# Attention, gated product and routed experts in one kernel: q and k transposed by head pairs, scores on half-array rows, and moved steps in the opening and around the last routing

## The chip, the cores and the metric

The kernel runs on one core of one Trainium2 chip. The metric is device time in microseconds (us), from the start of one execution to its end; the reference's arithmetic is all done in one launch.

## What is computed

Three blocks follow one another, in f32: attention with a sliding window of 128 and four sink tokens (4 batches, 8 heads, 768 tokens, head size 64), a gated product, and eight experts of which each token uses one.

```python
keep = (pos_k < 4) | ((rel >= 0) & (rel < 128))          # sinks, or inside the window
a = softmax(where(keep, q @ k.T / sqrt(64), -1e9))        # (4, 8, 768, 768)
x = (a @ v) as (3072, 512)                                # heads side by side
x = (((x @ w1) * (x @ w2)) @ w3) @ w_out                  # 512 -> 1024 -> 1024 -> 512; weights are f64
e = argmax(x @ w_gate + modality_bias[modality_id])       # one of 8 experts a token
out = gate * (relu(x @ e_w1[e]) @ e_w2[e])                # 512 -> 1024 -> 512
```

## The kernel before

All products keep f32 accuracy by a split: a number is a high part in f32r and a low part (what is left), and a product is high x high, high x low and low x high, three matmuls of 512 columns where one would stand. The five engines are TensorE (PE), VectorE (DVE), ScalarE (ACT), GpSimd (POOL) and SyncE (SP), which issues most transfers.

**Opening** (`front`, `startup_stream`). The f64 weights come in through SP into four tiles `f64st` (`f64_load`), DVE turns them into f32 (`f64_to_f32`), PE transposes w3 (L280), ACT and a correction matmul with `neg_r` split the result (`split_bank`, L266 to L268), and PE multiplies w3 by w_out into eight tiles `w3o` (L289). Attention steps are put between.

**Attention.** The work is 48 pairs n: 12 units u of 256 tokens (batch b, chunk c of 3) by 4 head pairs p. For each pair:
- `a_load`, `a_load_v`: q, k and v from DRAM;
- `a_split`: ACT makes the high parts of q and k, DVE the low parts, in SBUF;
- `a_tq`, `a_tk` (L396, L415): for each of head and half unit PE transposes a 128x128 block that holds high and low part side by side, so that high and low lie on rows 0 to 63 and 64 to 127; `a_swap` writes a second q with the two exchanged;
- `a_scores(n, j)` for the two half units j: two matmuls of 264 columns a head (two blocks of 128 keys and 4 sinks), with q and swapped q, over all 128 rows (L441). DVE masks and takes the maximum, ACT the exponential, `norm` (DVE) divides;
- `a_sk`: POOL collects the sink columns in `psk` and PE transposes them (L492);
- `a_pt`: PE transposes the probabilities in f32 (L504), ACT evicts, POOL masks;
- `a_pv`: PE multiplies by v in f32, 64 output columns a head (L531; an f32 matmul is two passes in the trace), adds the sinks (L534), and ACT and DVE split the result into `xb`.

**moe1_stream** runs six groups `gr` of two units: `ab` products (L703, w1 and w2, 16 groups of 12 matmuls), `x2` products (L691), and the `late` half of them. `front` puts attention steps of the next group between its steps, by a model time t, and steps of `route` (16 reductions on DVE, L764, then the expert's choice, its rank, and the tables) for the units already done. In the last group attention is over, and the slots of the experts start: a `Slot` is 512 tokens of one expert; `decide` picks it on DVE (some 16 small operations) and SP loads the result into registers, since the addresses of the slot's weights and tables depend on it.

**back** works the slots off: `stage1` (L912), `stage2` (L949), the weight pieces of the next slot (`w1_piece`, `w2_piece`: SP load L868 or L870, split on ACT L195 and DVE L196) and its transposes (L899).

The order of the instructions of an engine follows from the code's order and from a scheduler, which moves an instruction up where it judges its operands ready; `high_priority` moves a stretch forward. Each engine then works its own list in order.

Of the kernel before, what the change touches and what calls it, by code (L numbers as in the profile page):

```python
# [26 lines left out]
def attention_moe_moe_kernel(ctx, tc, q, k, v, w1, w2, w3, w_out, mod_id, w_gate, mod_bias, e_w1, e_w2, out,  # L27
# [18 lines left out]
    banded = n_sink == NS and window == 128  # L46

# [46 lines left out]
    neg_r = const.tile([128, 128], F32R, name="neg_r")  # L94
    cur_i = const.tile([128, 128], I32, name="cur_i")
# [12 lines left out]
    ksk = const.tile([128, H, NS], F32R, name="ksk")  # L108
# [3 lines left out]
    def consts_early():  # L112
# [5 lines left out]
        nc.vector.tensor_scalar(out=neg_r, in0=idf, scalar1=-1.0, scalar2=None, op0=ALU.mult)  # L118
        nc.gpsimd.memset(tmp, 1.0)
# [217 lines left out]
    carry = {}  # L337
    xb = mm.tile([128, NP, 2, 3, UNIT], F32R, tag="xb", bufs=1, name="xb")

    def a_load(n):  # L340
# [3 lines left out]
        qn = att.tile([128, 2, 2, D], F32, tag="qn", bufs=2, name="qn")  # L344
        kn = att.tile([128, 2, 2, D], F32, tag="kn", bufs=2, name="kn")
        for src, dst in ((q, qn), (k, kn)):
            for j in range(2):
                s0 = c * UNIT + j * 128
                nc.sync.dma_start(out=dst[:, :, j], in_=src[b, hs, s0:s0 + 128, :].rearrange("h s d -> s h d"))
        nat[n] = (qn, kn)  # L350

    def a_load_v(n):
# [8 lines left out]
        if c == 0 and p == 0:  # L361
            for kind in range(3):
                for h in range(2):
                    r = kind * 32 + h * NS
                    nc.sync.dma_start(out=vst[r:r + NS, :, h * D:(h + 1) * D],
                                      in_=v[b].rearrange("(p h) s d -> h s p d", h=2)[h, 0:NS])
# [7 lines left out]
    def a_split(n):  # L374
        qn, kn = nat.pop(n)
        qs = att.tile([128, 4, 2, D], F32R, tag="qs", bufs=1, name="qs")
        ks = att.tile([128, 4, 2, D], F32R, tag="ks", bufs=1, name="ks")
        qf = qn.rearrange("p h j d -> p (h j) d")
        kf = kn.rearrange("p h j d -> p (h j) d")
        nc.scalar.activation(out=qs[:, :, 0, :], in_=qf, func=ACTF.Copy, scale=1.0 / float(D) ** 0.5)  # L380
        nc.scalar.activation(out=ks[:, :, 0, :], in_=kf, func=ACTF.Copy)

        def low_parts():
            nc.vector.scalar_tensor_tensor(out=qs[:, :, 1, :], in0=qf, scalar=1.0 / float(D) ** 0.5,
                                           in1=f32(qs[:, :, 0, :]), op0=ALU.mult, op1=ALU.subtract)
# [23 lines left out]
    def a_tk(n):  # L409
# [9 lines left out]
        if c == 0:  # L419
            nc.gpsimd.tensor_copy(out=ksk[:, 2 * p:2 * p + 2, :], in_=f32(kT[:, :, 1, NS:2 * NS]))  # L420
# [794 lines left out]
```

## Time and profile before

| | us |
|---|---|
| median of 3 runs (1012.55 to 1014.28) | 1012.94 |
| the profiled execution | 1017.59 |
| its span | 1015.9 |

| engine | busy, us | share of the span | instructions |
|---|---|---|---|
| PE, matmuls | 956.0 | 94% | 4976 |
| PE, weight loads (beside matmuls) | 752.5 | 74% | 4976 |
| DVE | 644.0 | 63% | 1968 |
| ACT | 515.8 | 51% | 1354 |
| POOL | 218.0 | 21% | 460 |

Busy time is the union of an engine's instructions. A matmul's record is longer than what it costs: the next one starts before it ends, so the cost of a group is read from start to start. Whose wait ends last is told by the view of waits; an idle engine that nobody waits for costs nothing.

### The profile page before, as it was taken

Reading aid. Unit: us, or ns where it says so; the run is one execution under the profiler, and the core shown is the slowest. Engines: PE = TensorE matmul, PEld = TensorE weight load, DVE = VectorE, ACT = ScalarE, POOL = GpSimd, SP = SyncE. Lnnn points to the kernel's source line nnn. Section 1 sums busy time; section 2 is a strip of 40 time slices with the busy share of each in tenths; the row PEclk is TensorE's granted clock in tenths of the full one; section 3 lists DMA queues with packets and bytes.
Section 4 is the critical chain, followed back from the end, with each engine's and each line's share of the span. In section 5 each row is a group of like instructions: output and inputs, shape, how many; then the busy total and the mean of one; then the engine's idle time right before and its main releaser. Section 6 shows DMA issues by size and latency. Waiting matters only on the chain. (4 is left out here: it accounts for less than half of the span.)

```text
span 1015.9 us, 16038 instructions
## 1 busy us (share of the span) xinstructions
PE 956.0 (94%) x4976; PEld 752.5 (74%) x4976; DVE 644.0 (63%) x1968; ACT 515.8 (51%) x1354; POOL 218.0 (21%) x460
## 2 busy tenths in 40 slices
PE   4899799999999999999999999999999997999995
PEld 2667578867786778678867886778888886888884
DVE  7788796489638963895489639847934354343432
ACT  3689665576447644774576445314433414343433
POOL 1232312113223221222122222222031222021010
PEclk9899999999999999999999999999999998999998
DMA  8665624112202220222022200452445306343331
GB/s 262 188 171 167 188 69 131 23 45 63 58 19 49 58 55 19 56 61 52 16 50 59 58 9 16 129 80 63 145 166 117 133 13 236 125 146 117 122 116 52
DMA packets 125417, 94.05 MB, mean 93 GB/s; under 512 B 96712, under 2 KB 105160, under 8 KB 125201
## 3 DMA queue, kind: packets, MB, share of 16 engines
q1 hardware_dynamic: 120560, 80.12, 28.3%
q0 software_dynamic: 4768, 12.88, 4.2%
q8 instruction: 40, 0.66, 0.3%
q14 instruction: 49, 0.39, 0.2%
HBM read 80.14 MB, written 13.09 MB: 92 GB/s over the span
## 5 line engine op out<-in xcount | busy, mean ns | idle before, releaser
L703 PE MATMUL ab<-xb,wab 128*128 128x512 f32 x1152 | 291.0, 397 | 0.4 <-DVE g L713 0.3
L703 PEld LDWEIGHTS ab<-xb,wab 128*128 128x128 f32 x1152 | 210.6, 189 | 41.9 <-ACT xb L537 1.2
L949 PE MATMUL x<-w 128*128 128x512 f32 x600 | 143.1, 396 | 0.0
L764 DVE CUSTOM_DVE_ANT_0 junk<-rows,wgb 128x512 bf16<-128x512 f32 x192 | 134.8, 702 | 1.5 <-ACT rows L751 0.6
L949 PEld LDWEIGHTS x<-w 128*128 128x128 f32 x600 | 113.1, 190 | 23.7 <-DVE w L196 0.3
L691 PE MATMUL x2p<-w3o,gh 128*128 128x512 f32 x384 | 128.2, 407 | 0.0
L461 ACT ACTIVATE P<-sp,st 128x132 f32<-128x132 f32 (+1 forms) x192 | 69.2, 368 | 40.4 <-DVE st L459 26.4
L196 DVE TENSOR_TENSOR w<-wst,w 128x512 fp32r<-128x512 f32 x112 | 71.5, 683 | 25.1 <-ACT w L195 25.1
L513 POOL TENSOR_SCALAR_AFFINE_SELECT ptp<-ptf 128x512 f32<-128x512 f32 (+1 forms) x96 | 63.7, 688 | 107.8 <-ACT ptf L508 107.8
L691 PE MATMUL x2p<-w3o,gl 128*128 128x512 f32 x192 | 76.4, 400 | 0.0
L691 PEld LDWEIGHTS x2p<-w3o,gh 128*128 128x128 f32 x384 | 66.9, 188 | 11.8 <-ACT gh L680 1.9
L912 PE MATMUL ab<-w,w 128*128 128x512 f32 x288 | 75.1, 396 | 0.0
L916 DVE SCALAR_TENSOR_TENSOR w<-ab,w 128x512 fp32r<-128x512 f32 x48 | 33.1, 690 | 65.6 <-ACT w L915 65.4
L195 ACT ACTIVATE w<-wst 128x512 fp32r<-128x512 f32 x112 | 63.5, 628 | 20.9 <-DMA wst<-in_moe_w_dram 20.9
L912 PE MATMUL ab<-w 128*128 128x512 f32 x288 | 74.0, 392 | 0.0
L953 POOL DMA_INDIRECT out_dram<-late,ti x25 | 25.6, 1026 | 217.1 <-ACT late L952 193.0
L680 ACT ACTIVATE gh<-g 128x256 fp32r<-128x256 f32 x96 | 39.9, 415 | 63.0 <-DVE g L710 48.1
L710 DVE TENSOR_TENSOR g<-ab,bs 128x256 f32<-128x256 f32 x48 | 20.2, 421 | 76.6 <-PE ab L703 76.5
L485 POOL CAST psk<-P 128x16 fp32r<-128x16 f32 (+1 forms) x96 | 23.7, 276 | 202.1 <-DVE P L468 149.6
L915 ACT ACTIVATE w<-ab 128x512 fp32r<-128x512 f32 x48 | 28.8, 599 | 74.5 <-PE ab L912 74.1
L912 PEld LDWEIGHTS ab<-w,w 128*128 128x128 f32 x288 | 54.0, 188 | 13.0
L912 PEld LDWEIGHTS ab<-w 128*128 128x128 f32 x288 | 54.0, 188 | 12.1
(195 smaller groups left out, 1685.7 us busy)
## 6 DMA issues: line engine op xcount, KB each, us to landing
wst<-in_moe_w_dram SPq DMA_DIRECT2D x56, 512.0 KB
f64st<-in_moe_w_dram SPq DMA_DIRECT2D x32, 512.0 KB
vn<-in_v_dram SPq DMA_DIRECT2D x128, 64.0 KB
xs<-rows SPq DMA_DIRECT2D x12, 513.0 KB
qn<-in_q_dram SPq DMA_DIRECT2D x96, 64.0 KB
kn<-in_k_dram SPq DMA_DIRECT2D x96, 64.0 KB
f64st<-in_moe_w_out_dram SPq DMA_DIRECT2D x8, 512.0 KB
wgb<-wgt SPq DMA_DIRECT2D x1, 2048.0 KB
```

The lines of the kernel that those rows point to most:

```text
L195: nc.scalar.activation(out=hi, in_=src, func=ACTF.Copy)
L196: lo_eng.tensor_tensor(out=lo, in0=src, in1=f32(hi), op=ALU.subtract)
L461: nc.scalar.activation(out=P[:, j, h, lo:KW], in_=sp[:, h, lo:KW], func=ACTF.Exp, bias=st[:, 0, h:h + 1], accum_out=st[:, 1, h:h + 1])
L513: nc.gpsimd.affine_select(out=parts[:, a, i0:2].rearrange("p j h q -> p (j h) q"), in_=full[:, 2 * i0:4], pattern=[[0, 4 - 2 * i0], [sign, ...
L680: nc.scalar.activation(out=gh, in_=g, func=ACTF.Copy)
L691: nc.tensor.matmul(out=x2p[t], lhsT=a[:, sl], rhs=b_, start=(f == 0 and i == 0), stop=(f == KF - 1 and i == 2))
L703: nc.tensor.matmul(out=bank[nm].rearrange("p (u t) -> p u t", u=2), lhsT=a, rhs=b_, start=(kk == 0 and i == 0), stop=(kk == KD - 1 and i = ...
L764: nc.vector.tensor_tensor_reduce(out=junk, in0=rows[:, t, 0:DM], in1=wgb[0][:, e, :], scale=1.0, scalar=0.0, op0=ALU.mult, op1=ALU.add, ac ...
L912: nc.tensor.matmul(out=hp, lhsT=a[:, fs], rhs=b_, start=(kk == 0 and i == 0), stop=(kk == KD - 1 and i == 2))
L915: nc.scalar.activation(out=h[:, 0], in_=hp, func=ACTF.Relu)
L916: nc.vector.scalar_tensor_tensor(out=h[:, 1], in0=hp, scalar=0.0, in1=f32(h[:, 0]), op0=ALU.max, op1=ALU.subtract)
L949: nc.tensor.matmul(out=op, lhsT=a[:, ts], rhs=b_, start=(f == 0 and i == 0), stop=(f == KF - 1 and i == 2))
```

## The change

- q and k of a pair are transposed unsplit, both heads at once: four f32 transposes instead of eight (`a_tqk`), so that head 0 lies on rows 0 to 63 and head 1 on rows 64 to 127. The split happens on the way out of PSUM: ACT writes the high parts, DVE (for n of at least 8) or a correction matmul and ACT (for the first 8, `n < FEW`) the low parts. `a_split`, `a_swap`, the swapped q and the copies `carry` and `ksk` are gone; k blocks lie in a ring of three.
- A score call is six matmuls of 264 columns (132 for the first block of a batch) over 64 rows each, the two heads in turn.
- For the first 8 pairs ACT divides the probabilities, and a correction matmul and ACT make the low part of `xb`.
- The sink transposes are a step of their own (`a_skT`), behind the next pair's `a_tqk`.
- q, k and v of the first two pairs are loaded ahead of the weight tiles that wait for a free `f64st`; attention starts with more steps a weight step.
- In the last group the routing steps are spread like in the others, three decisions come later, and in `back` three more decisions come one slot later in the code.

```diff
+    QDIV = float(D) ** 0.5
+    FEW = 2 * NP if math.frexp(QDIV)[0] == 0.5 else 0
...
-        qn = att.tile([128, 2, 2, D], F32, tag="qn", bufs=2, name="qn")
+        qn = att.tile([128, 2, 2 * D], F32, tag="qn", bufs=3, name="qn")
...
+    def a_tqk(n):
...
+        tp = ps_t.tile([128, 4, 128], F32, tag="t", name="tqk")
+        for x, src in enumerate((qn, kn)):
+            for j in range(2):
+                i = j if x == 0 or s0 < s1 else 1 - j
+                nc.tensor.matmul(out=tp[:, 2 * x + i], lhsT=src[:, j], rhs=idf, is_transpose=True, start=(x + j == 0),
+                                 stop=(x + j == 2), skip_group_check=True)
...
+        nc.scalar.activation(out=qh, in_=tp[:, 0:2], func=ACTF.Copy, scale=scale)
+        nc.scalar.activation(out=kr[:, 0, blocks, NS:KW], in_=tp[:, 2:4], func=ACTF.Copy)
+
+        def low_parts():
+            if n < FEW:
+                nc.tensor.matmul(out=tp[:, 0:2], lhsT=negq_r, rhs=qh, start=False, stop=True, skip_group_check=True)
+                nc.tensor.matmul(out=tp[:, 2:4], lhsT=neg_r, rhs=kr[:, 0, blocks, NS:KW], start=False, stop=True,
+                                 skip_group_check=True)
+                nc.scalar.activation(out=ql, in_=tp[:, 0:2], func=ACTF.Copy, scale=scale)
+                nc.scalar.activation(out=kr[:, 1, blocks, NS:KW], in_=tp[:, 2:4], func=ACTF.Copy)
+                sinks()
+                return
+            nc.vector.scalar_tensor_tensor(out=ql, in0=tp[:, 0:2], scalar=scale, in1=f32(qh), op0=ALU.mult,
+                                           op1=ALU.subtract)
+            nc.vector.tensor_tensor(out=kr[:, 1, blocks, NS:KW], in0=tp[:, 2:4], in1=f32(kr[:, 0, blocks, NS:KW]),
+                                    op=ALU.subtract)
+            sinks()
...
-        for h in range(2):
-            for part in range(2):
-                nc.tensor.matmul(out=sp[:, h, 0:2 * KW], lhsT=stt["q", n, part][:, 2 * h + j, :],
-                                 rhs=kT[:, h, s0:s0 + 2, :].rearrange("p a b -> p (a b)"),
-                                 start=(part == 0), stop=(part == 1))
+        for i, (a, b_) in enumerate(((qh, 0), (ql, 0), (qh, 1))):
+            for h in range(2):
+                hp = slice(h * D, (h + 1) * D)
+                nc.tensor.matmul(out=sp[:, h, 0:nk].rearrange("p (a b) -> p a b", b=KW), lhsT=a[hp, j, :],
+                                 rhs=kr[hp, b_, blocks, :], start=(i == 0), stop=(i == 2))
...
+            if n < FEW:
+                for h in range(2):
+                    nc.scalar.activation(out=P[:, j, h, lo:KW], in_=P[:, j, h, lo:KW], func=ACTF.Copy,
+                                         scale=r[:, h:h + 1])
+                return
...
+        if n < FEW:
+            nc.tensor.matmul(out=xp[:, 0], lhsT=neg_r, rhs=xh, start=False, stop=True, skip_group_check=True)
+            nc.scalar.activation(out=xl, in_=xp[:, 0], func=ACTF.Copy)
...
             if n + 1 < NN:
-                a_tq(n + 1)
-                a_swap(n + 1)
+                a_tqk(n + 1)
+            if n:
+                a_skT(n - 1)
             yield
...
-        f64_ahead(4)
+        with tc.high_priority(offset=400):
+            f64_ahead(2)
+            if banded:
+                a_load(0)
+            f64_ahead(4)
+            if banded:
+                a_load(1)
+                a_load_v(0)
...
-                att_upto(min(0.75 * (i + 1), 8) + 38 * t / 46700)
+                att_upto(min(1.5 * (i + 1), 14) + 32 * t / 46700)
...
-                early += [(20000 + 3000 * i, next_early) for i in range(N_EARLY - 1)]
+                early += [(47000 + 1500 * i, next_early) for i in range(N_EARLY - 1)]
...
-                    due = min(t, 18000) / 420
+                    due = min(t, 46000) / 1100
...
-            if pos == N_EARLY - 2:
-                while route_step():
-                    pass
...
+                    if pos == N_EARLY - 1 and f == 2:
+                        while route_step():
+                            pass
+                        for x in range(N_LATE + 1):
+                            slots.append(Slot(SLOT if x < N_LATE else 128, NT, mem))
+                            slots[-1].decide()
```

In the tables of order below a row is a line of the code, the operation, output<-inputs and shape; `x12` is twelve in a row.

PE in the attention stretch, before: a product with v, the transposes of k of the next pair, twelve `ab` matmuls and the first half of a score call.

```order
L531 MATMUL xp<-ptp,vn 64x256 x2
L531 MATMUL xp<-ptp,vn 64x128 x2
L534 MATMUL xp<-pskT,vsk 128x128
L415 MATMUL tk<-idr,ks 128x128 x4
L703 MATMUL ab<-xb,wab 128x512 x12
L441 MATMUL sp<-kT,qT 128x264
L441 MATMUL sp<-kT,qW 128x264
```

PE at the same place after, from the probabilities' transposes on: twelve `ab` matmuls, the paired transposes of the next pair, the sink transposes, six `x2` matmuls, a whole score call.

```order
L515 MATMUL pt<-idf,P 128x128 x4
L713 MATMUL ab<-xb,wab 128x512 x12
L395 MATMUL tqk<-idf,qn 128x128 x2
L395 MATMUL tqk<-idf,kn 128x128 x2
L503 MATMUL xp<-idr,psk 96x128
L701 MATMUL x2p<-w3o,gh 128x512 x2
L701 MATMUL x2p<-w3o,gl 128x512
L701 MATMUL x2p<-w3o,gh 128x512 x2
L701 MATMUL x2p<-w3o,gl 128x512
L442 MATMUL sp<-ring,qh 128x264 x2
L442 MATMUL sp<-ring,ql 128x264 x2
L442 MATMUL sp<-ring,qh 128x264 x2
```

The sink transposes, which stood right beside the probabilities' transposes, come behind twelve matmuls and a block of transposes, and a score call is one run of six, with full-row matmuls on both sides.

SP in the slots, before: the end of the register loads of the three late decisions (`dri`, `tri`) and the first weight load of slot 3 (L868).

```order
L840 TENSOR_LOAD dri
L840 ISA x2
L846 REGISTER_ALU
L846 DMA tk<-tab_70 128x1
L846 REGISTER_ALU
L846 DMA tk<-tab_71 128x1
L1168 TENSOR_LOAD tri
L1168 ISA x2
L868 ISA
L868 DMA wst<-in_moe_w_dram 128x1024
```

SP at the same place after: the last w1 load of slot 3 (L878), its first w2 load (L880), then the register loads.

```order
L878 ISA
L878 DMA wst<-in_moe_w_dram 128x1024
L880 ISA
L880 DMA wst<-in_moe_w_dram 128x2x512
L849 TENSOR_LOAD dri
L849 ISA x2
L850 TENSOR_LOAD dri
L850 ISA x2
```

The four w1 loads of slot 3 have gone ahead of the register loads; on DVE the decisions' operations stay behind the last stage-1 block of slot 2.

PE in the opening, before: the first attention matmuls (`tq`) stand behind the second block of w3 and six products.

```order
L280 MATMUL w3tp<-idf,w_286 128x128 x4
L267 MATMUL w3tp<-w3t,neg_r 128x512
L289 MATMUL w3o_acc<-wo,w3t 128x512 x6
L396 MATMUL tq<-idr,qs 128x128 x4
L289 MATMUL w3o_acc<-wo,w3t 128x512 x8
L415 MATMUL tk<-idr,ks 128x128 x4
L289 MATMUL w3o_acc<-wo,w3t 128x512 x4
```

PE at the start after: transposes of the first pair behind the first two weight tiles, two correction matmuls (`negq_r`, `neg_r`), and the first score call behind ten products.

```order
L284 MATMUL w3tp<-idf,w_169 128x128 x4
L395 MATMUL tqk<-idf,qn 128x128 x2
L395 MATMUL tqk<-idf,kn 128x128 x2
L271 MATMUL w3tp<-w3t,neg_r 128x512 x2
L293 MATMUL w3o_acc<-wo,w3t 128x512 x6
L405 MATMUL tqk<-qh,negq_r 128x256
L406 MATMUL tqk<-ring,neg_r 128x256
L293 MATMUL w3o_acc<-wo,w3t 128x512 x4
L442 MATMUL sp<-ring,qh 128x132 x2
```

The first pair's transposes have moved ahead of all products of w3 and w_out, and correction matmuls stand between them and the scores.

## Rows read from the trace of the kernel before

**Rows 1.** Stretches: length, busy of PE, PEld, DVE, ACT, POOL, granted clock, DMA, GB/s.

```profile
0.00:129.40 129.40, 103.53 (x565) 76.81 (x566) 103.56 (x255) 86.77 (x230) 31.69 (x74) 0.96 0.64 191
129.40:640.00 510.60, 496.87 (x2813) 385.24 (x2811) 358.95 (x1229) 295.37 (x877) 119.94 (x300) 1.00 0.20 49
660.90:664.30 3.40, 3.16 (x12) 2.58 (x12) 3.05 (x23) 0.60 (x1) 2.79 (x3) 0.50 0.40 30
846.20:852.00 5.80, 5.79 (x18) 4.92 (x19) 4.33 (x7) 3.63 (x8) 2.42 (x3) 0.50 0.90 321
```

**Rows 2.** What PE waited for, 129.4 to 640 us: total, times, longest.

```profile
PE xp L492 <- POOL psk L488: 7.6, 18, 1.1
```

**Rows 3.** What PE waited for from 640 us to the end.

```profile
PE x L899 <- DVE w L196: 5.6, 1, 5.6
PE rk L786 <- DVE oh L775: 2.6, 1, 2.6
```

**Rows 4.** PE's timeline, 178 to 200 us: start, length, line, operands, count.

```profile
178.43 0.28 PE L441 MATMUL sp<-kT,qT 128*128 128x264 f32 x1
...
178.91 2.91 PE L703 MATMUL ab<-xb,wab 128*128 128x512 f32 x12
...
183.64 0.46 PE L396 MATMUL tq<-idr,qs 128*128 128x128 f32 x4
183.93 2.97 PE L703 MATMUL ab<-xb,wab 128*128 128x512 f32 x12
...
196.73 0.60 PE L504 MATMUL pt<-idf,P 128*128 128x128 f32 x4
197.09 3.02 PE L703 MATMUL ab<-xb,wab 128*128 128x512 f32 x12
```

**Rows 5.** PE's timeline around products with v, 190 and 305 us.

```profile
190.06 1.09 PE L531 MATMUL xp<-ptp,vn 128*64 128x256 f32 x12
...
305.08 0.62 PE L691 MATMUL x2p<-w3o,gh 128*128 128x512 f32 x2
305.54 0.40 PE L691 MATMUL x2p<-w3o,gl 128*128 128x512 f32 x1
305.87 0.65 PE L531 MATMUL xp<-ptp,vn 128*64 128x256 f32 x2
306.44 0.74 PE L691 MATMUL x2p<-w3o,gh 128*128 128x512 f32 x2
```

**Rows 6.** L531 in all, then from 305 to 307 us: min/median/max ns.

```profile
L531 PE MATMUL xp<-ptp,vn x512: 272/273/431, 48.6 to 638.6; 128*64 128x128 f32 x109, 128*64 128x256 f32 x62
...
L531 PE MATMUL xp<-ptp,vn x2: 379/404/430, 305.9 to 306.1; 128*64 128x256 f32 x2
```

**Rows 7.** Timeline of PE's weight loads, 305.9 us.

```profile
305.87 0.19 PEld L531 LDWEIGHTS xp<-ptp,vn 128*64 128x64 f32 x2 [0.36 <-issue]
```

**Rows 8.** DVE's groups in the opening: count, busy us, mean ns, idle before.

```profile
L468 DVE TENSOR_TENSOR P<-P,st 128x264 f32<-128x264 f32 (+1 forms) x17 | 7.2, 424 | 0.2
...
L384 DVE SCALAR_TENSOR_TENSOR qs<-qn,qs 128x256 fp32r<-128x256 f32 x10 | 5.1, 514 | 0.0
L386 DVE TENSOR_TENSOR ks<-kn,ks 128x256 fp32r<-128x256 f32 x10 | 4.3, 427 | 0.0
```

**Rows 9.** ACT's groups in the opening.

```profile
L406 ACT ACTIVATE qW<-tq 64x512 fp32r<-64x512 f32 x20 | 11.9, 594 | 0.2
...
L418 ACT ACTIVATE kT<-tk 128x256 fp32r<-128x256 f32 x18 | 6.2, 392 | 2.6 <-PE tk L415 2.5
```

**Rows 10.** PE's timeline at the start.

```profile
7.36 1.08 PE L280 MATMUL w3tp<-idf,w 128*128 128x128 f32 x4 [7.36 <-DVE w L188]
```

**Rows 11.** Timeline of DVE and SP's transfers around slot 3's weight loads.

```profile
823.70 0.17 DVE L812 TENSOR_SCALAR dw<-dec 128x8 f32<-128x8 f32 x1
...
831.30 0.15 DVE L1167 CAST tri<-tro 128x1 int32<-128x1 f32 x1
...
836.94 7.36 SPq L868 DMA_DIRECT2D wst<-in_moe_w_dram  x4
```

More of the change, by code (lines that the diff above doesn't have):

```diff
@@ L94, in attention_moe_moe_kernel @@
     neg_r = const.tile([128, 128], F32R, name="neg_r")
+    negq_r = const.tile([128, 128], F32R, name="negq_r")
     cur_i = const.tile([128, 128], I32, name="cur_i")
@@ L372, in a_vsink @@
         stt["vsk", b] = vsk
[L374 to L385, printed above, removed]
-            nc.vector.tensor_tensor(out=ks[:, :, 1, :], in0=kf, in1=f32(ks[:, :, 0, :]), op=ALU.subtract)
-        stt["low", n] = defer(low_parts)
-        stt["s", n] = (qs, ks)
@@ L391, in a_tq @@
-    def a_tq(n):
-        qs, ks = stt["s", n]
-        stt.pop(("low", n))()
-        tp = ps_t.tile([128, 4, 128], F32R, tag="t", name="tq")
-        for i in range(4):
-            nc.tensor.transpose(out=tp[:, i, :], in_=qs[:, i].rearrange("p a d -> p (a d)"), identity=idr)
-        qT = att.tile([128, 4, 128], F32R, tag="qT0", bufs=2, name="qT")
-        nc.scalar.activation(out=qT, in_=f32(tp), func=ACTF.Copy)
-        stt["q", n, 0] = qT
-        stt["tq", n] = tp
-    def a_swap(n):
-        qW = att.tile([128, 4, 128], F32R, tag="qT1", bufs=2, name="qW")
-        tp = stt.pop(("tq", n))
-        for x in range(2):
-            nc.scalar.activation(out=qW[x * D:(x + 1) * D], in_=f32(tp[(1 - x) * D:(2 - x) * D]), func=ACTF.Copy)
-        stt["q", n, 1] = qW
@@ L434, in a_scores @@
         b, c = divmod(u, NC)
[L435 removed]
+        if j == 0:
+            stt.pop(("low", n))()
+        kr = ring[p]
+        qh, ql = stt["q", n]
         sp = ps_s.tile([128, 2, 512], F32, tag="s", name="sp")
+        cur = (2 * c + j) % 3
         blk0 = c == 0 and j == 0
[L438 to L443 removed]
+        wrapped = cur == 0 and not blk0
+        blocks = slice(0, 1) if blk0 else slice(0, 3, 2) if wrapped else slice(cur - 1, cur + 1)
+        nk = KW if blk0 else 2 * KW
+        for i, (a, b_) in enumerate(((qh, 0), (ql, 0), (qh, 1))):
[3 more added lines that the diff above has]
+                                 rhs=kr[hp, b_, blocks, :], start=(i == 0), stop=(i == 2))
         if j == 0:
@@ L491, in a_sk, with a_skT @@
                                     op=ALU.subtract)
+    def a_skT(n):
+        c = n // NP % NC
+        j0 = 0 if c else 1
+        xp = ps_x.tile([128, 2, 256], F32, tag="x", name="xp")
+        stt["x", n] = xp
+        for j in range(j0, 2):
             nc.tensor.transpose(out=xp[0:96, 1, j * 128:(j + 1) * 128].bitcast(F32R), in_=psk[:, j, :], identity=idr)
```

107 lines of the change are left out of this document (49 added, 58 removed).

## The prediction

> **What bounds the kernel now.** I read the stretches by stage first, then TensorE's waits, then its timeline where the change touches it. TensorE (PE below) works 496.9 of the 510.6 us of the attention stretch (129.4 to 640 us) [rows 1], so an instruction put on PE or taken off it counts there nearly in full, and anything else counts only where PE waits for it. The opening (weights converted from f64, first eight pairs of attention; to 129.4 us, when the first mixture matmul starts) is different: 103.5 us of PE work beside 103.6 us of VectorE (DVE) work, so 26 us of PE idle [rows 1]. Of the 13.7 us idle in the attention stretch, 7.6 us in 18 waits are the sink transposes of L492 waiting for GpSimd (POOL) [rows 2]. Behind it stand two single stalls: 2.6 us for the routing's one-hot (L786) and 5.6 us for a split (L899) [rows 3]. After each of the two the granted clock is 0.50 (1.2 of 2.4 GHz) for a while, 3.4 and 5.8 us [rows 1].
>
> The profiled execution took 1017.6 us around a span of 1015.9; the median of the runs is 1012.9. The terms come from the one execution and are taken off the median, since its 0.5% more does not sit in one stage that I can name.
>
> **Transposes.** Before, a pair has two blocks of four (L396, L415); after, one block of four (a_tqk), in f32 as L504 has it. A block's cost is start to start plus what the matmuls behind it lose: twelve L703 matmuls take 2.91 us undisturbed (one alone 0.40 [rows 5], so 0.23 apart); the L396 block takes 0.29 us and the twelve behind it 2.97, so 0.35 us; the L504 block takes 0.36 and the twelve behind it 3.02, so 0.47 [rows 4]. A pair saves 2 x 0.35 - 0.47 = 0.23 us, and 40 of the 48 lie behind the opening: **-9 us**.
>
> **Scores.** This term decides. Before, a call issues four matmuls of 264 columns over all 128 rows, 0.48 us from its first to the next L703 [rows 4], 0.12 each. After, six, each over 64 rows: head 0 on rows 0 to 63, head 1 on rows 64 to 127, into two PSUM banks, in turn. No row of the trace has a matmul on half the rows. The nearest are L531's, on half the columns (one head each). Those run side by side: a call with c > 0 has four passes of 256 and eight of 128 columns; the shortest pass is 379 ns long with 256 columns and 272 with 128 [rows 6], so 107 ns for 128 columns and 1.71 us for all passes in turn, and they take 1.09 us [rows 5]. But they pay at both ends. A lone two passes of 256 columns start 0.33 us behind the matmul ahead (usual 0.23), the next start comes 0.57 us later where two passes need 0.43, and the two matmuls behind take 0.74 instead of 0.62: 0.10 + 0.14 + 0.12 = 0.36 us [rows 5]. The weight load shows it: it begins at 305.87 together with its matmul, after 0.36 us in which no weights were loaded [rows 7]. I take the half-row calls to behave so: three couples of 0.12 us, plus 0.36, plus 0.05 because 128 weight columns instead of 64 are loaded in the open (half of 0.107) = 0.77 us against 0.48. In units with c = 0 the j = 0 call has 132 columns, but a weight load of 0.107 us then sets its pace, so little comes off: +0.28 on average. 80 calls behind the opening: **+22 us**. The ends: no price, 3 x 0.12 - 0.48 = -0.12 (-10 us); no overlap and no price, 6 x 0.12 - 0.48 = +0.24 (+19 us); no overlap and the price, +0.65 (+52 us). I take +22 because these rows are the only ones where the array is divided, and both halves of the reading come from them.
>
> The Trainium skill (TensorEngine Tiling (Array Packing), Key Properties) says that changing the tiling mode, and not just the tile, drains TensorE, and that tiles work independently. The column rows bear out both (0.36 us; 1.09 for 1.71), and no row shows it for half rows; by that rule the term is +22, without it -10.
>
> **Sink transposes.** They move out of a_sk into a step of their own behind the next pair's transposes. In the changed program's order twelve matmuls and a block of transposes now stand between (2.75 us at 0.23), while the 18 waits were 0.4 us each on average and 1.1 at the longest [rows 2]. The 7.6 us go; I leave 1 us for the low parts of q and k, which now hold the PSUM bank that L504 needs until DVE has read it: **-6.5 us**.
>
> **Opening.** A pair takes from DVE two normalisations (424 ns), the low parts of q (514) and k (427) [rows 8], 1.8 us, and by my estimate 0.8 more for the xb subtraction and the carry copies, of the same 256 columns: 2.6 x 8 = 21 of its 103.6 us. ScalarE (ACT) takes these over: three evictions of 256 columns (392 ns) and four normalisations half as long, 7 x 392 = 2.7 us at most; it loses the swap (2 x 594) and the separate q eviction, splits and one of two kT evictions (392 or more each) [rows 9]: about even. PE gets three correction matmuls of 256 columns, each between 0.12 (half of 0.23) and 0.37 (with a start behind ACT), I take 0.25: 24 x 0.25 = 6 us; 16 score calls at 0.28 add 4.5, the transposes take off 8 x 0.23 = 1.8. So DVE falls to 83 us, PE rises to 112, and PE can't start before the first converted tile, at 7.36 us [rows 10]: 120 us instead of 129.4 if the denser chain (correction matmul behind ACT, ACT behind it) leaves no idle. Ends: 0 and -10; I take **-7 us**, since PE's 103.5 counts lone matmuls at full length, which overlap once it is denser. The q, k, v of the first two pairs now go ahead of two f64 loads of 512 KB on SP's queue; that delays the second pair of weight tiles, and DVE's spare 20 us cover it.
>
> **Last group and slots.** The routing of the last group spreads over 46 instead of 18 model-us, so DVE no longer runs behind at L786: -2.6, and half of the 3.4 us at half clock: **-4.3**. The early decisions come some 25 model-us later; two and the loop count took 7.75 us of DVE [rows 11], and two now stand between the last two products of moe1, 30 matmuls (6.9 us) apart: about even, at worst +2. The stall at L899 is one of SP's queue: the weight loads of slot 3 (L868) stand behind the register loads of three decisions, whose last DVE step ends at 831.45, and are issued at 836.94 [rows 11]. After, they stand ahead of the decisions, and three w2 loads, wanted only after eight stage-1 blocks, stand behind: -5.6, and half of 5.8 us at half clock: **-8.5**.
>
> **Sum.** -9 + 22 - 6.5 - 7 - 4.3 - 8.5 = -13.3; 1012.9 - 13.3 = **999.6 us**.
>
> **The rivals.** *Free division*: half-row calls join the stream without a price and run in couples. Nothing in the trace shows it; against it, every lone half-column call pays. Scores -10 instead of +22, and the opening gains 3 more: 999.6 - 35 = 965.
> *In turn, without a price*: scores +19: 997. Against it stands the overlap of the column halves.
> *In turn, with the price*: this one ends on the other side. Both heads write all 128 partitions of PSUM, which L531's halves don't; if the write side takes one stream at a time, a call is 6 x 0.12 + 0.41 = 1.13 us, the scores +52, and the opening loses 5 of its 7: 999.6 + 30 + 5 = 1035. The other terms are -35 in all, so the change is slower from a call of 0.48 + 35 / 80 = 0.92 us on. The Trainium skill (TensorE: Matmul & The Clock Gate, Part 3) gives 3.07 times the speed for four row tiles of 512 columns, which speaks against it; no run here shows that.
> *The stalls only move*: opening, sinks and slots give half: 999.6 + 11 = 1011.
>
> **How the numbers follow.** The forecast has 0.50, free division 0.22, in turn without price 0.12, in turn with price 0.09, stalls that only move 0.07. The forecast's own range is 989 to 1011 (opening 0 to -10, 0.05 us either way on a call, small terms). To hold 8 in 10 the range must take in free division and can leave out 1035: 960 to 1012. About 0.2% (2 us) is what a measurement of this kernel can tell from no change. Faster: 0.45 of the forecast's 0.50, 0.22, 0.11 and 0.02 of the last, 0.80; same 0.05; slower 0.15.
>
> **What would show it.** In the changed trace a score call takes 0.7 to 0.8 us from its first start to the next L713, and its first weight load is not ahead of its matmul; 0.36 means free division, 1.1 the slow rival. L503 is gone from PE's waits, the first L713 starts near 122 us with DVE under 90 us to there, and neither the routing matmuls nor L909 show a wait over 1 us or a clock of 0.50 behind them. The forecast is wrong if the score calls differ, or if the opening still ends at 129 because ACT's chain has become the wait.

## The result and the profile after

The changed kernel takes **1001.23 us** (1000.07 to 1003.18, 4 runs) beside 1013.24 (1012.55 to 1014.28, 4 runs) for the kernel before: ratio 0.9883, 95% interval 0.9864 to 0.9901. The forecast was 999.6 us and "faster" with a chance of 0.80; the interval lies below 1, and 12.0 us came off where 13.3 were expected. The sum was better than its terms, as the stages show. They are cut at the first mixture matmul, at the same matmuls of the groups, and at the first matmuls of the slots; "before, again" is a second profiled execution of the unchanged kernel:

| stage, us | before | before, again | after |
|---|---|---|---|
| opening | 129.3 | 122.6 | 126.3 |
| groups 0 to 4 (attention beside them) | 503.2 | 502.6 | 505.1 |
| group 5 | 76.2 | 74.0 | 70.2 |
| slot 2 | 54.6 | 53.2 | 45.9 |
| everything else | 252.6 | 252.6 | 251.6 |
| span | 1015.9 | 1005.0 | 999.2 |

The two executions of before (1017.59 and 1006.67 us) stand on either side of their median, and neither is typical (sixteen other runs of before took 1010.67 to 1016.02); so a stage's gain is read against both.

After, windows (length, busy of PE, PEld, DVE, ACT and POOL with counts, granted clock, DMA share, GB/s), to be read against [rows 1]; the third is where before stood at half clock behind the one-hot:

```profile
0.00:126.28 126.28, 107.42 (x583) 76.05 (x584) 85.82 (x202) 80.42 (x235) 25.56 (x64) 0.96 0.66 196
126.28:633.00 506.72, 494.76 (x2797) 364.87 (x2797) 349.89 (x1163) 205.89 (x686) 109.91 (x262) 1.00 0.21 48
660.00:664.00 4.00, 4.00 (x20) 3.30 (x19) 0.00 (x0) 0.60 (x1) 0.46 (x1) 1.00 0.27 78
...
120.00:124.00 4.00, 4.00 (x17) 2.86 (x16) 2.09 (x6) 0.86 (x3) 0.64 (x2) 0.57 0.33 67
```

DVE lost 17.7 us of the opening's work and PE gained 3.9, yet PE is still idle for 18.9 us there, and near its end the clock falls to 0.57.

After, PE's waits (total, times, longest): the first two from 126 to 633 us, the last the only one from there to the end. It answers [rows 2, 3]:

```profile
PE xp L503 <- POOL psk L492: 7.6, 15, 0.8
PE pt L515 <- DVE P L474: 2.4, 4, 0.7
...
PE x2p L701 <- ACT gh L690: 0.5, 1, 0.5
```

The two single stalls of [rows 3] are gone. The sink transposes (L492 before, L503 now) wait exactly as long as before.

After, PE's timeline (start, length, line, operands, count) around a block of transposes and a score call, to be read against [rows 4]:

```profile
180.76 0.38 PE L395 MATMUL tqk<-idf,qn 128*128 128x128 f32 x2
180.98 0.38 PE L395 MATMUL tqk<-idf,kn 128*128 128x128 f32 x2
181.12 0.37 PE L503 MATMUL xp<-idr,psk 128*96 128x128 f32 x2
181.32 2.99 PE L713 MATMUL ab<-xb,wab 128*128 128x512 f32 x12
...
183.69 0.61 PE L713 MATMUL ab<-xb,wab 128*128 128x512 f32 x2
184.24 0.39 PE L442 MATMUL sp<-ring,qh 64*128 64x264 f32 x2
184.47 0.28 PE L442 MATMUL sp<-ring,ql 64*128 64x264 f32 x2
184.59 0.28 PE L442 MATMUL sp<-ring,qh 64*128 64x264 f32 x2
184.79 1.88 PE L713 MATMUL ab<-xb,wab 128*128 128x512 f32 x7
```

After, its weight loads there:

```profile
184.24 0.19 PEld L442 LDWEIGHTS sp<-ring,qh 64*128 64x128 f32 x2 [0.35 <-issue]
```

The two heads of a couple run side by side: six matmuls in three couples, 0.12 us apart once they flow. The first weight load begins with its matmul, after 0.35 us without one. The price lies at both ends: the call starts 0.33 us behind the start of the matmul ahead (usual 0.23), and the seven matmuls behind it take 1.88 us where 6 x 0.23 + 0.39 = 1.77 are usual. From the first start to the next L713 are 0.55 us, 0.76 with the two ends, against 0.50 for an undisturbed call of before counted in the same way (median of 54 there, 59 here).

### The profile page after: what moved, and what is told of

It is laid out like the page before. It is cut to its first block, busy times and chain, and to the rows that moved or that the text cites. A ratio compares the mean times of both kernels' runs of the same rounds, so it can differ in the third digit from the quotient of the medians.

```text
span 999.2 us, 15565 instructions
## 1 busy us (share of the span) xinstructions
PE 956.1 (96%) x5000; PEld 730.3 (73%) x5000; DVE 619.3 (62%) x1865; ACT 420.2 (42%) x1170; POOL 207.6 (21%) x412
## 5 line engine op out<-in xcount | busy, mean ns | idle before, releaser
L713 PE MATMUL ab<-xb,wab 128*128 128x512 f32 x1152 | 288.4, 397 | 0.0
L713 PEld LDWEIGHTS ab<-xb,wab 128*128 128x128 f32 x1152 | 209.9, 188 | 44.1 <-issue 0.4
L959 PE MATMUL x<-w 128*128 128x512 f32 x600 | 141.0, 392 | 0.0
L774 DVE CUSTOM_DVE_ANT_0 junk<-rows,wgb 128x512 bf16<-128x512 f32 x192 | 138.7, 722 | 3.2 <-ACT rows L761 1.8
L489 POOL CAST psk<-P 128x16 fp32r<-128x16 f32 (+1 forms) x96 | 28.9, 330 | 275.5 <-DVE P L474 138.7
L524 POOL TENSOR_SCALAR_AFFINE_SELECT ptp<-ptf 128x512 f32<-128x512 f32 (+1 forms) x96 | 65.8, 708 | 94.7 <-ACT ptf L519 94.3
L200 DVE TENSOR_TENSOR w<-wst,w 128x512 fp32r<-128x512 f32 x112 | 71.3, 685 | 10.6 <-ACT w L199 10.6
L442 PE MATMUL sp<-ring,qh 64*128 64x264 f32 (+1 forms) x384 | 61.0, 331 | 2.4 <-ACT P L462 1.2
```

The source lines that it names most:

```text
L200: lo_eng.tensor_tensor(out=lo, in0=src, in1=f32(hi), op=ALU.subtract)
L442: nc.tensor.matmul(out=sp[:, h, 0:nk].rearrange("p (a b) -> p a b", b=KW), lhsT=a[hp, j, :], rhs=kr[hp, b_, blocks, :], start=(i == 0), st ...
L524: nc.gpsimd.affine_select(out=parts[:, a, i0:2].rearrange("p j h q -> p (j h) q"), in_=full[:, 2 * i0:4], pattern=[[0, 4 - 2 * i0], [sign, ...
L713: nc.tensor.matmul(out=bank[nm].rearrange("p (u t) -> p u t", u=2), lhsT=a, rhs=b_, start=(kk == 0 and i == 0), stop=(kk == KD - 1 and i = ...
L774: nc.vector.tensor_tensor_reduce(out=junk, in0=rows[:, t, 0:DM], in1=wgb[0][:, e, :], scale=1.0, scalar=0.0, op0=ALU.mult, op1=ALU.add, ac ...
L959: nc.tensor.matmul(out=op, lhsT=a[:, ts], rhs=b_, start=(f == 0 and i == 0), stop=(f == KF - 1 and i == 2))
```

## Experiments: the score call

**Head by head.** The six matmuls of a call in another order:

```diff
-        for i, (a, b_) in enumerate(((qh, 0), (ql, 0), (qh, 1))):
-            for h in range(2):
+        for h in range(2):
+            for i, (a, b_) in enumerate(((qh, 0), (ql, 0), (qh, 1))):
```

> The changed kernel with the six matmuls of a score call in another order: three of head 0, then three of head 1, so that no two neighbours use different row halves except at the change of head. If couples overlap (my theory), a call goes from 0.76 us to about 0.76 + 3 x 0.12 = 1.1 us, some 32 us in all over 96 calls, about 1033 us, a little less if the two heads overlap at the change. If the two heads run in turn in any case, nothing changes (1001).

Measured: 1002.9 us (1001.51 to 1003.76), ratio to before 0.9906 [0.9891, 0.9921]: no change from 1001.2. PE's timeline of it, the same call:

```profile
184.50 0.40 PE L442 MATMUL sp<-ring,qh 64*128 64x264 f32 x2
184.73 0.29 PE L442 MATMUL sp<-ring,ql 64*128 64x264 f32 x2
184.85 0.29 PE L442 MATMUL sp<-ring,qh 64*128 64x264 f32 x2
185.06 1.66 PE L713 MATMUL ab<-xb,wab 128*128 128x512 f32 x6
```

The program issues all three matmuls of head 0 first, yet in time they run in couples: head 1's first matmul starts 10 ns behind head 0's first (4 ns in the interleaved kernel), while head 0's second and third, which stand ahead of it, still wait. My expectation that the order makes the couples is refuted. Here each half of the array took its next matmul without waiting for those of the other half that stood ahead of it in the program, up to three of them. The Trainium skill (TensorEngine Tiling (Array Packing), Key Properties) says that different tiles can load weights and multiply in parallel; this pair of traces agrees, and shows that the order need not help them.

**Four full rows.** The price by itself: four matmuls over 128 rows, as many as before had. The scores' values are not the reference's, since each matmul sums both heads and one product of the split is left out.

```diff
-        for i, (a, b_) in enumerate(((qh, 0), (ql, 0), (qh, 1))):
+        for i, (a, b_) in enumerate(((qh, 0), (ql, 1))):
...
-                hp = slice(h * D, (h + 1) * D)
+                hp = slice(0, 2 * D)
...
-                                 rhs=kr[hp, b_, blocks, :], start=(i == 0), stop=(i == 2))
+                                 rhs=kr[hp, b_, blocks, :], start=(i == 0), stop=(i == 1))
```

> The changed kernel with four score matmuls a call over all 128 rows, as many and as long as before the change (each sums both heads, so scores are wrong and one product of the split is left out; everything else stays). It prices the score term alone, read in the attention stretch, since other scores may route tokens otherwise and change the slots. By clean calls 0.48 for 0.76, so -0.28 x 80 = -22 us between the opening's end and the first slot matmul (575.4 us after). Rival: the old call's true price was higher (its mean in the trace is nearer 0.58 with its waits), because the chain into it is long; if those waits come back with the short call, the gain is only about 12 us.

Measured: 976.94 us, 0.9632 [0.9604, 0.966], 24.3 us under the changed kernel. PE's timeline of one call:

```profile
195.25 0.40 PE L442 MATMUL sp<-ring,qh 128*128 128x264 f32 x2
195.49 0.41 PE L442 MATMUL sp<-ring,ql 128*128 128x264 f32 x2
195.74 0.62 PE L701 MATMUL x2p<-w3o,gh 128*128 128x512 f32 x2
```

From the first start to the next product are 0.49 us, with nothing to pay at the ends. Groups 0 to 4 take 486.9 instead of 505.1 us, although a stall of 3.9 us (the one of the next section) has come into them: 18.2 + 3.9 = 22.1 us for 80 calls, 0.28 a call. That is the size of the forecast's term. The expectation had named the stretch up to the first slot, which is 16.3 us shorter; the rest is the 3.9 us and 1.9 us that group 5 takes more (other scores, other tokens routed: not followed further).

## Experiments: the opening

**Before, profiled again.** The unchanged kernel.

> The kernel before, unchanged, profiled a second time. Its first profiled execution took 1017.6 us against a median of 1013.2; the changed kernel's profile differs from it by 16.7 us, the medians by 12.0. If the first profile held a stage that is dear only sometimes, this one is nearer 1013 and the stage shows: first suspects are the stretch of slot 2 (54.6 us, with the stall at L899) and the last group's first part (60.2 us, with the stall at L786). If both stages are as long again, the 4.7 us are spread evenly or are the difference of a profiled and an unprofiled execution.

Measured: 1006.67 us, with the opening of 122.6 us in the table above, 6.8 less than in the profile that the prediction read. What differs is in the main one wait. The timeline of the first execution, POOL's sink columns and PE behind them (in brackets the idle time before, and who ended it):

```profile
116.05 1.53 POOL L485 CAST psk<-P 128x16 fp32r<-128x16 f32 x2 [7.09 <-DVE P L468]
117.55 3.95 POOL L488 TENSOR_TENSOR psk<-P,psk 128x8 fp32r<-128x8 f32 x2
...
121.39 0.50 PE L492 MATMUL xp<-idr,psk 128*96 128x128 f32 x2 [4.91 <-POOL psk L488]
```

The second execution, POOL alone:

```profile
114.72 0.57 POOL L485 CAST psk<-P 128x16 fp32r<-128x16 f32 x2 [6.54 <-DVE P L468]
115.26 0.98 POOL L488 TENSOR_TENSOR psk<-P,psk 128x8 fp32r<-128x8 f32 x2
```

A subtraction of 8 columns took 3.78 us of the 3.95 in one execution and 0.37 in the other. In the second execution both subtractions were done when a small DVE instruction (L466) followed the first of two splits. In the first execution POOL's second copy was held up to that point, and the subtraction met the run of seven conversions and splits behind it, up to DVE's next small instruction at 121.2. The changed kernel has the same event in the profile. Its timeline: a pair of POOL's copies elsewhere, then the opening's, then PE behind it, and DVE in the meantime:

```profile
156.79 0.33 POOL L489 CAST psk<-P 128x16 fp32r<-128x16 f32 x2 [1.57 <-PE ab L713]
...
115.80 3.34 POOL L489 CAST psk<-P 128x16 fp32r<-128x16 f32 x2 [11.67 <-ACT P L471]
119.12 0.35 POOL L492 TENSOR_TENSOR psk<-P,psk 128x8 fp32r<-128x8 f32 x2
...
119.36 0.42 PE L503 MATMUL xp<-idr,psk 128*96 128x128 f32 x2 [2.53 <-POOL psk L492]
...
115.79 0.42 DVE L186 TENSOR_SCALAR w<-f64st 128x512 uint32<-128x512 uint32 x1
116.12 0.69 DVE L200 TENSOR_TENSOR wab<-w,wab 128x512 fp32r<-128x512 f32 x1
116.73 0.68 DVE L189 SCALAR_TENSOR_TENSOR w<-f64st,w 128x512 uint32<-128x512 uint32 x1
117.33 0.42 DVE L186 TENSOR_SCALAR w<-f64st 128x512 uint32<-128x512 uint32 x1
117.66 0.69 DVE L192 SCALAR_TENSOR_TENSOR w<-f64st,w 128x512 uint32<-128x512 uint32 x1
118.26 0.69 DVE L189 SCALAR_TENSOR_TENSOR w<-f64st,w 128x512 uint32<-128x512 uint32 x1
118.87 0.17 DVE L467 TENSOR_SCALAR st<-st 128x2 f32<-128x2 f32 x1
```

Two copies take 0.33 us where DVE does nothing. Here the first lasts as long as DVE's run of six conversions and splits without a gap, and ends when a small instruction follows. It was so in three more traces: 3.8 us beside seven such DVE instructions in the first execution of before, 4.4 and 4.2 us beside eight in the runs with no work moved and with four full rows. Over the whole trace of the changed kernel, 53 of these small POOL instructions had no DVE instruction beside them and took 186 to 207 ns (one of them 248). Those with nothing but reductions and masks of the scores in PSUM beside them (L460, L454) took 189 to 203; of the seven beside L200, with two inputs in SBUF, one took 191 and the others 497 to 3212. The Trainium skill (SBUF — State Buffer, Who interferes with whom) says that a DVE instruction with two SBUF inputs contends with a GpSimd instruction that reads SBUF, that `tensor_scalar` can too in some modes, and that the ports they share are an exclusive lock. The rows agree, and show more: POOL did not get in between the six. PE then waits 2.5 us and falls to 0.57 of its clock for the next 4 us (120 to 124 us in the windows above).

**Fewer steps early.** The old number of attention steps in the opening:

```diff
-                att_upto(min(1.5 * (i + 1), 14) + 32 * t / 46700)
+                att_upto(min(0.75 * (i + 1), 8) + 38 * t / 46700)
```

> The changed kernel with the old number of attention steps per weight step in the opening (0.75 a step up to 8, then 38 over the rest). If starting attention early fills PE's holes before 30 us, this costs 2 to 3 us (opening to 129 us). If the wait of 3.8 us for ACT at the first probabilities' transposes (28.4 us) comes from starting too early, it is gone here and the time is the same or 2 us less.

Measured: 995.25 us, 0.9824 [0.981, 0.9838], **6.0 us under the changed kernel**; the opening ends at 121.6 us. The part of the change that was meant to start more attention early costs time, and neither reading of mine was the reason. With fewer early steps POOL's last copies of the opening fall beside other work, and none is slow (POOL's timeline):

```profile
112.22 0.80 POOL L489 CAST psk<-P 128x16 fp32r<-128x16 f32 x2 [6.42 <-ACT P L471]
```

**Sinks later.** The sink transposes one step further back:

```diff
-            if n:
-                a_skT(n - 1)
             yield
-            a_scores(n, 1); yield
+            a_scores(n, 1)
+            if n:
+                a_skT(n - 1)
+            yield
```

> The changed kernel with the sink transposes one step later still, behind the second score call. If what is left of the waits (7.6 us behind the opening, nearly all in the late parts of the groups, where steps follow each other fast) is POOL's lag behind the division, one more step takes most of it: 995 to 998 us. If it is a chain that moves along (the product with v then waits for the evicted sinks), 1001 and the waits stand at L542 or L545.

Measured: 995.77 us, 0.9832 [0.9819, 0.9846], 5.5 us under. The timeline, POOL and PE:

```profile
115.07 3.34 POOL L489 CAST psk<-P 128x16 fp32r<-128x16 f32 x2 [11.48 <-ACT P L471]
...
118.64 0.43 PE L503 MATMUL xp<-idr,psk 128*96 128x128 f32 x2 [0.26 <-POOL psk L492]
```

The copy is as slow as in the changed kernel, 3.34 us, but PE has other work until 118.6 and waits 0.26 us. The opening ends at 121.9. Behind it nothing changed: the sink transposes still wait 7.3 us in 14 places. So the time lies in the range that I gave, but not for the reason I gave: the gain is the stall in the opening, and the 7.6 us that the edit was meant for are still there.

**Both.** The two edits together:

> Two edits together, each of which alone took about 6 us off the changed kernel (995.3 and 995.8 against 1001.2 us): the old number of attention steps in the opening, and the sink transposes behind the second score call of the next pair. Theory A, one stall: both cure the same wait. In the profile of the changed kernel PE waits 2.5 us near 117 us for the sink columns, because one small GpSimd copy lasts 3.2 us there beside a dense run of VectorE's f64 conversions, and PE falls to half clock behind it (0.57 from 120 to 124 us); both edits have the opening end at 121.6 to 121.9 us instead of 126.3. Then the two together give no more than the better one, 993 to 996 us. Theory B, two gains: the steps and the sinks each save their own work and add up, 1001.2 - 6.0 - 5.5 = 989.7 us, with an opening that ends near 117 us.

Measured: 996.12 us (992.95 to 996.66, 5 runs), 0.9825 [0.9806, 0.9844]; the opening ends at 121.7. The gains do not add up: both edits remove one stall, the one by a copy that is not slow, the other by work in front of the wait, and with either one the kernel is some 6 us faster than the changed one and 18 faster than before. With the sinks later, the two numbers of early steps take the same time (995.77 and 996.12): the early steps cost only through the stall, and gain nothing by themselves.

**No work moved to PE and ACT.** `FEW = 0`, so the first eight pairs go through DVE like the others:

```diff
-    FEW = 2 * NP if math.frexp(QDIV)[0] == 0.5 else 0
+    FEW = 0
```

> The changed kernel without the special treatment of the first eight pairs: DVE makes the low parts and the divisions there too, and the 24 correction matmuls fall away. The opening ended at 126.3 us instead of the forecast 122. If DVE's load was what bound the opening, it goes back to 129 or later (about +3 us, 1004). If ACT's chain has become the wait, taking its work away makes the opening shorter: 122 to 124 us (998).

Measured: 1002.25 us, 0.989 [0.9874, 0.9905]: no difference from 1001.2. The opening is 3.5 us shorter, 122.8, and the first group 4.0 longer. The stall has moved there, as POOL's timeline shows:

```profile
128.32 4.53 POOL L489 CAST psk<-P 128x16 fp32r<-128x16 f32 x2 [9.80 <-DVE P L474]
```

and PE's waits behind the opening:

```profile
PE xp L503 <- POOL psk L492: 3.5, 1, 3.5
```

In this opening PE waits 1.7 us for the sink columns at the longest. So three openings without the stall can be set side by side: this one, before again, and sinks later (windows):

```profile
0.00:122.75 122.75, 100.96 (x560) 71.47 (x561) 99.00 (x242) 64.84 (x180) 25.46 (x64) 0.96 0.68 198
...
0.00:122.56 122.56, 101.28 (x564) 74.70 (x565) 104.33 (x254) 86.70 (x230) 29.77 (x74) 0.99 0.66 196
...
0.00:121.92 121.92, 105.30 (x583) 74.95 (x584) 86.60 (x202) 80.86 (x235) 26.17 (x64) 0.97 0.67 200
```

DVE is busy for 99.0, 104.3 and 86.6 us, and the lengths differ by less than 1 us: taking that load off DVE, with some 4 us more of PE in its place, was worth no more than that.

**Division on DVE alone.**

```diff
-            if n < FEW:
+            if n < 0:
                 for h in range(2):
```

> The changed kernel with the division of the first eight pairs back on DVE (16 x 424 ns there instead of 32 operations of about 370 ns on ACT), the low parts staying on ACT and PE. DVE was busy 85.8 of the opening's 126.3 us and ACT 80.4, so if the wait of 3.8 us behind ACT's division at 28.4 us is what holds the opening up, it ends at 122 to 124 us here (998). If DVE still binds, it gets longer by 1 to 2 us.

Measured: 999.3 us, 0.9862 [0.9847, 0.9877], 1.9 under, about as much as the runs can tell. The opening ends at 124.9. The wait for the division is still there, 3.7 us behind DVE instead of 3.8 behind ACT, so where the division is done did not set it. The longest wait for POOL was 1.0 us here, so this gain may be the stall's.

**Loads in the old place.** The first q, k and v behind the four weight loads:

```diff
-        with tc.high_priority(offset=400):
-            f64_ahead(2)
-            if banded:
-                a_load(0)
-            f64_ahead(4)
-            if banded:
-                a_load(1)
-                a_load_v(0)
+        f64_ahead(4)
         if banded:
+            a_load(0)
+            a_load(1)
+            a_load_v(0)
             a_load_v(1)
```

> The changed kernel with the four first f64 loads again ahead of q, k and v of the first two pairs. By my account the second weight tiles come 1 to 2 us earlier and the first pair's transposes later; DVE has spare time for either, so within 1 us. If attention's early start hangs on these loads, the opening gets 2 to 4 us longer.

Measured: 1005.74 us, 0.9917 [0.9903, 0.9931] beside [0.9864, 0.9901] for the changed kernel: the loads ahead are worth 4.5 us by the medians, 3.4 by the ratios. The stall is there in both (2.8 and 2.5 us), and the first transposes of q start at 22.69 us instead of 10.05. This is the one part of the opening that pays beyond the runs' noise. The traces alone would not show it: its opening ends at 130.7 us, but one execution with the loads ahead reached 128.8 (in the run of the old routing times below).

## Experiments: sinks, the last routing, the slots

**Sinks in their old step.**

```diff
-                a_sk(n - 1); a_pt(n - 1); yield
+                a_sk(n - 1); a_skT(n - 1); a_pt(n - 1); yield
...
-            if n:
-                a_skT(n - 1)
             yield
```

> The changed kernel with the sink transposes back in the step of the probabilities' transposes. The forecast gave the move 6.5 us. The profile after shows PE still waiting 7.6 us for psk behind the opening, so the rival is that the move bought nothing there: then 1001 within 2 us and about the same total of waits. By the forecast 1007 to 1008, with 14 us or more of waits for psk.

Measured: 1007.92 us, 0.9952 [0.9939, 0.9966], 6.7 slower than with the move. PE's waits behind the opening:

```profile
PE xp L503 <- POOL psk L492: 13.6, 18, 1.4
```

The move takes these waits from 13.6 to 7.6 us, and groups 0 to 4 take 510.5 us without it instead of 505.1. (The rest of this profile's difference, 3.0 us, lies in the opening.) So the move is worth about what was forecast, but against a kernel that would have waited longer, not against the kernel before with its 7.6.

What still waits in the changed kernel is seen on PE's timeline:

```profile
229.85 0.38 PE L515 MATMUL pt<-idf,P 128*128 128x128 f32 x2
230.74 0.27 PE L503 MATMUL xp<-idr,psk 128*96 128x128 f32 x1 [0.50 <-POOL psk L492]
```

The sink transposes come straight behind those of the probabilities. It is so, with the transposes of P or another sink transpose directly ahead, in 14 of the 15 waits, and in all 14 of the run "Sinks later".

**Routing and decisions by the old times, in the last group.**

```diff
-                early += [(47000 + 1500 * i, next_early) for i in range(N_EARLY - 1)]
+                early += [(20000 + 3000 * i, next_early) for i in range(N_EARLY - 1)]
...
-                    due = min(t, 46000) / 1100
+                    due = min(t, 18000) / 420
```

> The changed kernel with the last group's old timing (routing steps within 18 model-us, early decisions from 20000 on). The forecast gave the new timing 4.3 us; the profile after has the last group's first part 6.8 us shorter, some of which is attention's tail. By the forecast 1005 to 1006 us, with the wait at the routing matmuls (2.6 us) and the stretch of 0.50 clock behind it back. Rival: the stall was a matter of one execution, then 1001.

Measured: 1001.93 us (1000.63 to 1005.46), 0.9882 [0.9858, 0.9905]: no difference that can be told. In its trace, PE's waits and the window behind them:

```profile
PE rk L796 <- DVE oh L785: 2.5, 1, 2.5
```

```profile
660.00:664.00 4.00, 3.94 (x22) 3.30 (x22) 3.57 (x26) 0.60 (x1) 3.01 (x3) 1.00 0.73 36
```

The wait is back, but the clock stays at 1.00, and group 5 takes 72.1 instead of 70.2 us: 1.9 us in the profile, of which the medians show 0.7 within their noise. (The profiled execution is the slowest of the six; another 2.5 us of it lie in the opening, which this edit does not touch.)

**Decisions of `back` in the old place.**

```diff
-                    if pos == N_EARLY - 1 and f == 2:
-                        while route_step():
-                            pass
...
+            if pos == N_EARLY - 2:
+                while route_step():
+                    pass
```

> The changed kernel with the three late decisions back at their old place in the code. By the forecast the stretch of slot 2 goes from 45.9 back to 54.6 us (5.6 us of wait for the split, and half of what runs at clock 0.50): 1009 to 1010 us. Rival: the changed order elsewhere keeps SP's queue clear, then 1001.

Measured: 1009.58 us, 0.9956 [0.994, 0.9973], 8.4 slower; slot 2 takes 54.3 instead of 45.9. SP's transfers, the four w1 loads of slot 3, first in the changed kernel, then in this run:

```profile
801.63 14.39 SPq L878 DMA_DIRECT2D wst<-in_moe_w_dram  x4
...
830.03 7.27 SPq L878 DMA_DIRECT2D wst<-in_moe_w_dram  x4
```

PE's waits there and the window behind:

```profile
PE x L909 <- DVE w L200: 5.8, 1, 5.8
```

```profile
838.00:848.00 10.00, 8.79 (x33) 7.42 (x34) 6.82 (x11) 5.71 (x11) 3.62 (x4) 0.69 0.90 310
```

## Why the prediction was right, step by step

- **Slots, -8.5: right.** Slot 2 lost 8.7 us against the first profile of before and 7.3 against the second, and undoing this one edit gave 8.4 back. The stall was one of SP's queue, as [rows 11] had it: the w1 loads of slot 3 are issued from 801.6 us on in the changed kernel, from 830.0 with the edit undone and from 836.9 before. The stretch at half clock went with it.
- **Scores, +22: right in mechanism and in the price of the new call, too large against the kernel before.** Couples run side by side, and a visit to the divided array is paid at both ends (0.10 ahead, 0.11 behind, no weight load in advance). The four full rows give 22.1 us for the 80 calls. The call costs 0.76 us (0.77 forecast), which excludes free division (0.36) and the call in turn with the price (1.13). In turn without a price would be 0.72, too near to be told by the cost; it is excluded by the starts, 4 ns apart within a couple. What the term had wrong is the old call: 0.48 us is an undisturbed one, and in the mean it cost 0.57, so that the calls took only some 12 us more (see groups 0 to 4). The test was worded wrongly: I asked for 0.7 to 0.8 us from the first start to the next L713, but a part of the price lies outside these two starts; in that count it is 0.55.
- **Transposes, -9: right**, somewhat small. A block of four f32 transposes cost 0.45 us (forecast 0.47) against twice 0.37, so -0.29 a pair and -11 in all.
- **Sink transposes, -6.5: the step failed** that took the waits of before as what the move removes. They stayed at 7.6 us [rows 2], and without the move they would have been 13.6. The prediction had twelve matmuls and a block of transposes between POOL's columns and the sink transposes. That is so in the stretch that I had looked at, but in 14 of the 15 places where PE still waits nothing stands between: a_skT's transposes follow right behind those of a_pt. Of the 7.6 us, 5.2 lie in the late parts of the groups and nearly all the rest in the first 8 us of a group. Why the waits would have grown to 13.6 no run isolates; a pair of the changed kernel has less work on PE, which may be the reason.
- **Opening, -7: the step failed** that read the gain off DVE's load. DVE fell to 85.8 us (83 forecast) and PE rose to 107.4 (112 forecast), but both kernels carry a wait that the load doesn't show. In the opening of the profile that I read, 4.9 us of PE's idle time were one wait for POOL's sink columns, and my rows on that wait began behind the opening. I wrote that the 0.5% by which this execution was slower sat in no stage that I could name; 6.8 of the 10.9 us between the two executions sit in the opening. The end at about 122 us was right for a changed kernel without the stall (121.6 to 121.9 in three runs), but before without it ends at 122.6, with DVE busy for 104.3 us: the openings without the stall differ by 1 us, not 7. The changed kernel has the stall and ends at 126.3. Of the opening's edits only the loads ahead show a gain (4.5 us when undone), and the steps early brought POOL's copy beside DVE's run (6.0 us less when undone).
- **Last group, -4.3**: the stage lost 6.0 us against one profile of before and 3.8 against the other, so the term has the right size there. But the edit of the times undone alone shows 0.7 by medians and 1.9 in the trace. The half clock behind the wait did not return, nor was it in the second execution of before (a wait of 1.7 us there, the clock at 1.00), so that half of the term was a property of one execution; the rest of the stage's gain probably belongs to the attention's end, whose waits of 1.1 and 0.8 us in this group are gone as well.
- **Groups 0 to 4**: forecast +6.5, measured +2.0 and +2.5 against the two profiles of before. With scores +22, transposes -11 and sinks 0 it would be +11. I summed all start-to-start gaps of PE from the first mixture matmul to the first slot by kind of matmul; what a gap between two products has above the usual 0.23 us went to the block of other matmuls beside it. By this sum the transposes of q and k took 16 us less, the sink transposes 3 more, and the score calls only 12 more (45 us before, 57 after). The old calls took 0.57 us in the mean, not the 0.50 of an undisturbed one: the 17 that stood directly ahead of products with v took 0.68 us up to them, and 3.0 us in all were waits, most for POOL's copies into kT. What else made them dear no run here isolates. In the run of four full rows the same sum is 15 us smaller at the calls, and 7 at the products with v and the transposes of P.

So the total came out close in part by luck. The opening was 4 us worse than forecast against one profile of before and 11 against the other, and the sink transposes wait as long as before; the old score calls, dearer than the 0.48 us of the forecast, made up for much of it, and the last group gained as much as forecast for other reasons in part. Two of the signs that the prediction asked for, L503 gone from the waits and an opening near 122 us, did not come. The slots were right for the reason given, the scores in mechanism and in the price of the new call.

## What to carry to other kernels

Profile the kernel before twice when its executions differ by more than the effect of a term, and look for the wait in which they differ before a gain is read from either. A tiny operation of GpSimd that TensorE waits for can last as long as VectorE's unbroken run beside it: put other work between it and its consumer, and see in the order of TensorE's instructions that the work really stands there. A visit to the divided array had a price at both ends here, which speaks for putting many half-row matmuls into one; the order of the halves within it did not matter. Price an old group of instructions by its mean in the trace, not by its best case.

## What was not expected of the hardware

- One copy of 128x16 on GpSimd took 3.2 us in the changed kernel (4.5 for the two copies in the kernel without moved work, beside eight DVE instructions), where it takes 0.2 alone: it was kept out not for one DVE instruction but for a gapless run of six.
- Matmuls on the two row halves start 4 to 10 ns apart even when three of one half are issued ahead of the first of the other.
- A wait of some 2.5 us on PE was followed by the low clock in some cases (0.57 at 120 to 124 us after, 0.50 behind L786 before) and not in two others: in the run with the old routing times, and in the run head by head behind the very same wait in the opening (window below, the wait ends at 120.8).

```profile
120.00:124.00 4.00, 3.19 (x20) 2.37 (x21) 1.54 (x6) 1.04 (x3) 2.09 (x6) 1.00 0.15 34
```
